# Window attention and two expert layers on one core: transposes of the last five tiles moved from TensorE to VectorE, late steps' square moved to ScalarE, new ranks for late work

## The chip, the cores and the metric

The kernel runs on one core of a Trainium2 chip. The time is that of one launch on the device in microseconds (us). Three runs of the kernel before gave 839.98, 840.34 and 841.68; 840.34 is their median. PE is TensorE, DVE VectorE, ACT ScalarE, POOL GpSimd, and SP the engine whose queue issues the DMA transfers. A core has one of each, each works through its own queue in order, and they wait for each other by semaphores.

## The reference

```python
def _attn_ref(q, k, v):                     # 4 x 8 x 576 x 64
    scores = scale * np.matmul(q, k.transpose(0, 1, 3, 2))
    mask = (rel >= 0) & (rel < 64)          # each query sees its own key and the 63 before
    scores = np.where(mask, scores, -1e9) - max
    attn = np.exp(scores); attn = attn / (attn.sum(-1) + 1e-09)
    return np.matmul(attn, v)

x = attn_out.transpose(0, 2, 1, 3).reshape(2304, 512)
h = x @ w_in; r = np.maximum(h, 0.0); x = (s * (r * r) + b) @ w_out    # 512 -> 2048 -> 512
h = x @ w_in2; out = np.maximum(0.01 * h, h) @ w_out2                  # 512 -> 2048 -> 512
```

The weights come as 64-bit floats, and the kernel turns their two 32-bit words into 32-bit floats itself.

## The kernel before, in words

*Attention.* The 2304 tokens are 18 tiles of 128. For a tile, TensorE computes the scores of two groups of four heads (`scores`, buffers sc), VectorE adds the mask and takes the row maximum (`mask_max`, eight instructions of 128 columns), ScalarE takes exp with the row sum (`exponent`), VectorE inverts the sum, and the rows are scaled (`normalise`). The result, called p, lies with queries on partitions (s, or in later tiles a part of the buffer vs). The product with v needs keys on partitions, so TensorE transposes p, four 128 x 128 blocks a group (`transpose_pe`, L285 to L288, into tp), ScalarE copies tp into pt (`take_transposed`, L290 to L296), and TensorE multiplies (`values`, L305, into xps). A tile's product stands in its queue whole (both groups next to each other) or in two halves.

*First layer.* Tokens are worked in blocks of 512, 512, 512, 512 and 256, and d_ff in 16 chunks of 128: 80 steps, each a pair of block and chunk. The first block's steps are cut in two runs of eight, with the second block's sixteen between them. Full precision comes from a split of every operand into a rounded high part and a remainder (h and l in the names: wh and wl, xh and xl, gh and gl) and three products of parts. A step has on TensorE twelve matmuls for h (`emit_h`, L532, into hps) and twelve for y (`emit_y`, L567, into acc, which gathers over the chunks in PSUM); between them come `activate` (L537 to L553): relu on ACT (L544, writes r), r = s*r*r on DVE (L546), gh = r + b rounded on ACT (L549), gl = r + b - gh on DVE (L551).

*Second layer.* Two levels of 2 x 2 blocks are multiplied with seven products each (L900, into xps, yps and zps), in three blocks of 768 tokens. Its weights are prepared during the first layer: 16 units (`add_weights2`, raw2 and flt2) are loaded, converted to 32-bit floats, summed and split on DVE and ACT, and stored to the DRAM buffers w1dr (first product) and w2dr (second), from which they are loaded again (ws).

*Order.* The program is written out by a planner (class `Order`): each operation has an engine, an estimated duration, the operations it waits for, the buffer rooms that it takes, and a key. Whenever a planned engine is free, the ready operation of the lowest key is emitted, so keys set the order in each queue. Keys are counted in steps: step s has keys near s, an attention tile has one key (L1157 for tiles 8 to 17) less an offset for each kind of operation, a weight unit of the second layer has STEPS1 - 10 or STEPS1 + 1 plus 0.1 for each unit (L1171; STEPS1 is 80). `fill` (L1122) puts matmuls of zeros (L1115, into warm or acc) where the planner sees TensorE idle in the first steps. What is in the queues is fixed when the program is built.

Of the kernel before, what the change touches and what calls it, by code (L numbers as in the profile page):

```python
# [9 lines left out]
F32 = mybir.dt.float32  # L10
# [116 lines left out]
def kernel(  # L127
# [82 lines left out]
    IN_W = (BLOCKS1[0] + BLOCKS1[1]) // P  # L210
    shared = {}
# [77 lines left out]

    def take_transposed(i, g):  # L290
        if i not in pt_t:
            pt_t[i] = (in_w("pt", [P, 2, H, D]) if i < IN_W
                       else tmpp.tile([P, 2, H, D], F32, tag="tmp", name="pt"))
        nc.scalar.activation(  # L294
            out=pt_t[i][:, :, 4 * g:4 * g + 4, :].rearrange("k a j q -> k j a q"),
            in_=tp_t[i, g].rearrange("k j (a q) -> k j a q", a=2), func=ACTF.Copy)  # L296
# [37 lines left out]
    def add_attention(i, b, t0, key):  # L334
# [3 lines left out]
        if i < IN_W:  # L338
            rq, rk, rv, first, rp = [mem("q")], [mem("k")], [mem("v")], [mem("s")], [mem("pt")]
            pt, after_v = ("pt", i), []  # L340
        else:
            rq, rk, rv, first, rp = [("q", "q", i)], [("k", "k", i)], [("big", "v", i)], [], [
                ("tmp", "pt", i)]
            pt, after_v = ("pt", i), [name("lv")]
# [15 lines left out]
        for g in range(2):  # L360
# [6 lines left out]
            for j in range(4):  # L367
                add(name("mm", g, j), "dve", 172, key - 4.87, lambda g=g, j=j: mask_max(i, g, j),
                    [name("sc", g)] + ([name("mm", 0, 0)] if g + j else after_v) + [("masks",)],
                    first if g + j == 0 else (), [("sc", i, j % 2), ss, ("sm", i)])  # L370
                add(name("exp", g, j), "act", 480, key - 3.07, lambda g=g, j=j: exponent(i, g, j),
                    [name("mm", g, j)], use=[ss, ("sm", i)])
# [12 lines left out]
            else:  # L385
# [4 lines left out]
            add(name("tp", g), "pe", 560, key - 2.96, lambda g=g: transpose_pe(i, g, tp),  # L390
                norm + [("masks",)], [(tp, "tp", i, g)], [ss])
            add(name("tt", g), "act", 478, key - 5.69, lambda g=g: take_transposed(i, g),
                [name("tp", g)] + ([name("tt", 0)] if g else []),
                [] if g else rp, [("tp", i, g), pt])
            last = [name("tt", g)]
# [140 lines left out]

    def activate(s, part):  # L537
        l, b, t0, n, c = steps[s]
        if part == 0:
            r_t[s] = gp.tile([P, NMAX], F32, tag="g", name="r")[:, :n]  # L540
            g_t[s] = tuple(gp.tile([P, NMAX], F32R, tag="g", name=t)[:, :n] for t in ("gh", "gl"))
        r, (gh, gl) = r_t[s], g_t[s]
        if part == 0:
            nc.scalar.activation(out=r, in_=hps_t[s], func=ACTF.Relu)  # L544
        elif part == 1:
            nc.vector.scalar_tensor_tensor(  # L546
                out=r, in0=r, scalar=sbt[:, 0:1], in1=r, op0=ALU.mult, op1=ALU.mult)
        elif part == 2:
            nc.scalar.activation(out=gh, in_=r, func=ACTF.Identity, bias=sbt[:, 1:2])  # L549
        else:  # L550
            nc.vector.scalar_tensor_tensor(  # L551
                out=gl, in0=r, scalar=sbt[:, 1:2], in1=gh.bitcast(F32), op0=ALU.add,
                op1=ALU.subtract)  # L553
# [49 lines left out]
    def add_step(s):  # L603
# [16 lines left out]
        add(("e", s, 1), "dve", 60 + 600 * f, s - 0.9, lambda: activate(s, 1),  # L620
# [518 lines left out]
    add(("masks",), "pool", 4000, -100, masks)  # L1139
    for c in range(KF):  # L1140
# [9 lines left out]
    for b, n in enumerate(BLOCKS1):  # L1150
        for j in range(n // P):
# [4 lines left out]
            else:  # L1156
                key = first_step[0, 2] - 10 + 2 * (i - IN_W)  # L1157
# [6 lines left out]
    for n, u in enumerate(units):  # L1164
# [6 lines left out]
        add_weights2(u, STEPS1 + (1 if u[1] else -10) + 0.1 * n, after)  # L1171
# [70 lines left out]
```

## Time and profile before

| | |
|---|---|
| median of three runs | 840.34 us |
| profiled execution, whole / span of its instructions | 838.37 / 836.6 us |
| granted TensorE clock, mean | 0.998 (of 2.4 GHz) |
| PE busy | 826.1 us, 99% |
| DVE busy | 600.5 us, 72% |
| ACT busy | 445.7 us, 53% |
| chain that ended last | PE 92%, DMA 2%, ACT 2%, DVE 2% |

The span runs from the first to the last instruction that the profiler shows; the execution is 1.8 us longer. Busy times of PE are from start to a modelled end, so two matmuls in a row overlap in them; what one costs is read from start to start. In the chain that ended last the matmuls of the first layer (L567 and L532) have 24% and 23%, those of the second (L900) 39%; the transposes of the tiles (L288) have 2% and their products with v (L305) 2%.

### The profile page before, as it was taken

Reading aid. Unit: us, or ns where it says so; the run is one execution under the profiler, and the core shown is the slowest. Engines: PE = TensorE matmul, PEld = TensorE weight load, DVE = VectorE, ACT = ScalarE, POOL = GpSimd, SP = SyncE. Lnnn points to the kernel's source line nnn. Section 1 sums busy time; section 2 is a strip of 40 time slices with the busy share of each in tenths; the row PEclk is TensorE's granted clock in tenths of the full one; section 3 lists DMA queues with packets and bytes.
Section 4 is the critical chain, followed back from the end, with each engine's and each line's share of the span. In section 5 each row is a group of like instructions: output and inputs, shape, how many; then the busy total and the mean of one; then the engine's idle time right before and its main releaser. Section 6 shows DMA issues by size and latency. Waiting matters only on the chain.

```text
span 836.6 us, 14149 instructions
## 1 busy us (share of the span) xinstructions
PE 826.1 (99%) x5289; PEld 735.7 (88%) x5289; DVE 600.5 (72%) x1095; ACT 445.7 (53%) x960; POOL 3.5 (0%) x13
## 2 busy tenths in 40 slices
PE   7999999999999999999999999999999999999998
PEld 4677888877777788888889999999999999999998
DVE  5999998556565756776878876699456688365963
ACT  5999655466776776443446433356332355222443
POOL 1000000000000000000000000000000000000000
PEclk9999999999999999999999999999999999999999
DMA  9763544438478564757388489899977898988783
GB/s 314 290 234 112 191 156 154 138 114 284 140 233 265 160 205 152 260 180 238 108 290 274 152 282 386 277 314 288 318 255 249 269 312 285 293 253 251 251 265 114
DMA packets 85909, 194.65 MB, mean 233 GB/s; under 512 B 7121, under 2 KB 50129, under 8 KB 81873
## 3 DMA queue, kind: packets, MB, share of 16 engines
q1 hardware_dynamic: 85840, 193.75, 69.7%
q8 instruction: 42, 0.69, 0.3%
q14 instruction: 27, 0.21, 0.1%
HBM read 151.26 MB, written 42.47 MB: 232 GB/s over the span
## 4 chain that ended last, share of the span: by engine, by line
PE 92%; DMA 2%; ACT 2%; DVE 2%; issue 1%; SPq 0%; ACTq 0%
PE acc L567 24%; PE hps L532 23%; PE xps L900 22%; PE zps L900 12%; PE yps L900 5%; PE xps L305 2%; PE sc L249 2%; PE tp L288 2%; DMA w2dr<-raw 1%; DMA x2l<-ydr 1%; DMA kt<-in_k 1%; PE warm L1115 1%; ACT pt L294 0%; DVE x2s L827 0%; ACT s L267 0%
## 5 line engine op out<-in xcount | busy, mean ns | idle before, releaser
L567 PE MATMUL acc<-gh,wh 128*128 128x512 f32 (+1 forms) x320 | 118.1, 375 | 0.0
L532 PE MATMUL hps<-xh,wh 128*128 128x512 f32 (+1 forms) x324 | 117.6, 370 | 0.1
L532 PE MATMUL hps<-xl,wh 128*128 128x512 f32 (+1 forms) x324 | 116.4, 367 | 0.0
L567 PE MATMUL acc<-gh,wl 128*128 128x512 f32 (+1 forms) x320 | 116.2, 369 | 0.0
L900 PE MATMUL xps<-x2h,ws 128*128 128x384 f32 x384 | 106.1, 334 | 0.4 <-ACT part L923 0.4
L796 ACT ACTIVATE g2s<-g 128x768 fp32r<-128x768 f32 x84 | 70.9, 847 | 64.0 <-PE xps L900 40.4
L923 ACT ACTIVATE part<-xps 128x384 f32<-128x384 f32 x90 | 44.1, 490 | 110.1 <-PE xps L900 110.0
L799 DVE TENSOR_TENSOR g2s<-g,g2s 128x768 fp32r<-128x768 f32 x84 | 80.1, 954 | 31.5 <-ACT g2s L796 30.7
L900 PE MATMUL xps<-g2s,ws 128*128 128x384 f32 x576 | 102.3, 334 | 0.1
L900 PEld LDWEIGHTS xps<-g2s,ws 128*128 128x128 f32 x576 | 99.9, 188 | 0.7 <-ACT part L923 0.7
L546 DVE SCALAR_TENSOR_TENSOR r<-r,sbt 128x512 f32<-128x512 f32 (+1 forms) x80 | 55.3, 691 | 44.0 <-ACT r L544 43.5
L567 PE MATMUL acc<-gl,wh 128*128 128x512 f32 (+1 forms) x320 | 86.1, 373 | 0.0
L544 ACT ACTIVATE r<-hps 128x512 f32<-128x512 f32 (+1 forms) x80 | 44.1, 551 | 78.6 <-PE hps L532 78.4
L532 PE MATMUL hps<-xh,wl 128*128 128x512 f32 (+1 forms) x324 | 80.6, 370 | 0.0
L551 DVE SCALAR_TENSOR_TENSOR gl<-r,sbt,gh 128x512 fp32r<-128x512 f32 (+1 forms) x80 | 55.5, 694 | 26.7 <-ACT gh L549 26.5
L532 PEld LDWEIGHTS hps<-xh,wh 128*128 128x128 f32 x324 | 61.1, 189 | 11.5 <-ACT wh L487 0.9
L900 PEld LDWEIGHTS xps<-x2h,ws 128*128 128x128 f32 x384 | 70.1, 188 | 0.7 <-ACT part L923 0.7
L567 PEld LDWEIGHTS acc<-gh,wh 128*128 128x128 f32 x320 | 60.3, 189 | 11.6 <-DVE st L594 0.7
L532 PEld LDWEIGHTS hps<-xl,wh 128*128 128x128 f32 x324 | 61.1, 189 | 9.8
L567 PEld LDWEIGHTS acc<-gh,wl 128*128 128x128 f32 x320 | 60.4, 189 | 9.4
L549 ACT ACTIVATE gh<-r,sbt 128x512 fp32r<-128x512 f32 (+1 forms) x80 | 54.0, 674 | 26.0 <-DVE r L546 26.0
L567 PEld LDWEIGHTS acc<-gl,wh 128*128 128x128 f32 x320 | 56.5, 189 | 10.7 <-issue 0.9
(93 smaller groups left out, 1395.9 us busy)
## 6 DMA issues: line engine op xcount, KB each, us to landing
ws<-w1dr SPq DMA_DIRECT2D x84, 512.0 KB, 4.6
ws<-w2dr SPq DMA_DIRECT2D x84, 512.0 KB, 4.6
raw<-in_w SPq DMA_DIRECT2D x31, 1024.0 KB, 5.1
w1dr<-raw SPq DMA_DIRECT2D x16, 512.0 KB, 5.0
w2dr<-raw SPq DMA_DIRECT2D x16, 512.0 KB, 4.1
kt<-in_k SPq DMA_DIRECT2D x14, 384.0 KB, 5.0
vs<-in_v SPq DMA_DIRECT2D x10, 512.0 KB, 3.8
out<-st SPq DMA_DIRECT2D x24, 192.0 KB, 4.2
```

The source lines that it names most:

```text
L249: nc.tensor.matmul(out=sc_t[i][r][D * a:D * a + D, p, :], lhsT=q_t[i][D * r:D * r + D, p, D * a:D * a + D], rhs=k_t[i][D * r:D * r + D, p, ...
L288: nc.tensor.transpose(tp_t[i, g][:, j, :], s_t[i][:, g, j, :], ident)
L532: nc.tensor.matmul(out=hps_t[s][:, c0:c1], lhsT=w[:, 0, kk * P:kk * P + P], rhs=x[l, b][:, kk, c0:c1], start=(kk == 0 and j == 0 and part ...
L544: nc.scalar.activation(out=r, in_=hps_t[s], func=ACTF.Relu)
L546: nc.vector.scalar_tensor_tensor(out=r, in0=r, scalar=sbt[:, 0:1], in1=r, op0=ALU.mult, op1=ALU.mult)
L549: nc.scalar.activation(out=gh, in_=r, func=ACTF.Identity, bias=sbt[:, 1:2])
L551: nc.vector.scalar_tensor_tensor(out=gl, in0=r, scalar=sbt[:, 1:2], in1=gh.bitcast(F32), op0=ALU.add, op1=ALU.subtract)
L567: nc.tensor.matmul(out=acc_t[r, m], lhsT=three[j][0], rhs=three[j][1], start=(c == c0 and j == 0), stop=(c == c1 - 1 and j == 2))
L796: nc.scalar.activation(out=out, in_=in_, func=ACTF.Copy)
L799: nc.vector.tensor_tensor(out=out, in0=in_, in1=hi.bitcast(F32), op=ALU.subtract)
L900: nc.tensor.matmul(out=out, lhsT=w_[:, wcut], rhs=x_, start=(opens and j == k == 0), stop=(j == n - 1 and k == 2), skip_group_check=not opens)
L923: nc.scalar.activation(out=t, in_=bank_t[(*key, "x")], func=ACTF.Copy)
```

## The change

Four things change. For tiles 13 to 17 (`BY_32 = 13`) p is transposed on VectorE: 24 instructions a tile, each of which transposes a strip of 32 queries by 32 keys for four heads, straight into one pt buffer that the five tiles share. The blocks that the mask leaves at zero aren't transposed; their places are set to zero once on POOL (`clear`). TensorE's transposes and ScalarE's copies of these tiles go. From step 46 on (`BY_ACT`) the square and the scale with offset are two ScalarE instructions, gh is a copy, and gl a plain subtraction on VectorE. Late tiles get other keys and other offsets of their operations, and the second layer's weight units too. The diff shows the new functions and each changed place.

```diff
@@ -281,6 +282,24 @@
...
+    def clear():
+        shared["pt"] = tmpp.tile([P, 2, H, D], F32, tag="tmp", name="pt")
+        for u in range(2):
+            nc.gpsimd.memset(shared["pt"][96 - 96 * u:128 - 96 * u, :, :, 32 * u:32 * u + 32], 0.0)
+    def transpose32(i, g, a, u, kb):
+        pt = pt_t[i] = shared["pt"]
+        q0 = D * a + 32 * u
+        nc.vector.transpose(
+            out=pt[32 * kb:32 * kb + 32, a, 4 * g:4 * g + 4, 32 * u:32 * u + 32],
+            in_=s_t[i][q0:q0 + 32, g, :, 32 * kb:32 * kb + 32])
@@ -365,10 +384,10 @@
...
-                add(name("mm", g, j), "dve", 172, key - 4.87, lambda g=g, j=j: mask_max(i, g, j),
+                add(name("mm", g, j), "dve", 172, key - (4.87 if early else 3.631), lambda g=g, j=j: mask_max(i, g, j),
-                add(name("exp", g, j), "act", 480, key - 3.07, lambda g=g, j=j: exponent(i, g, j),
+                add(name("exp", g, j), "act", 480, key - (3.07 if early else 3.369), lambda g=g, j=j: exponent(i, g, j),
@@ -387,12 +406,26 @@
...
-            add(name("tp", g), "pe", 560, key - 2.96, lambda g=g: transpose_pe(i, g, tp),
-                norm + [("masks",)], [(tp, "tp", i, g)], [ss])
-            add(name("tt", g), "act", 478, key - 5.69, lambda g=g: take_transposed(i, g),
-                [name("tp", g)] + ([name("tt", 0)] if g else []),
-                [] if g else rp, [("tp", i, g), pt])
-            last = [name("tt", g)]
+            if i < BY_32:
+                add(name("tp", g), "pe", 560, key - (2.96 if early else 2.594),
+                    lambda g=g: transpose_pe(i, g, tp),
+                    norm + [("masks",)], [(tp, "tp", i, g)], [ss])
+                add(name("tt", g), "act", 478, key - (5.69 if early else 1.5),
+                    lambda g=g: take_transposed(i, g),
+                    [name("tp", g)] + ([name("tt", 0)] if g else []),
+                    [] if g else rp, [("tp", i, g), pt])
+                last = [name("tt", g)]
+            else:
+                last = []
+                for u in range(2):
+                    for a in range(2):
+                        for kb in range(u, u + 3):
+                            n = name("t32", g, u, a, kb)
+                            add(n, "dve", 202, key - 7.437,
+                                lambda g=g, u=u, a=a, kb=kb: transpose32(i, g, a, u, kb),
+                                norm + [("clear",)]
+                                + [("pv", i - 1, h) for h in range(2) if i > BY_32], (), [ss, pt])
+                            last.append(n)
@@ -542,15 +578,24 @@
...
+        elif s < BY_ACT:
+            if part == 1:
+                nc.vector.scalar_tensor_tensor(
+                    out=r, in0=r, scalar=sbt[:, 0:1], in1=r, op0=ALU.mult, op1=ALU.mult)
+            elif part == 2:
+                nc.scalar.activation(out=gh, in_=r, func=ACTF.Identity, bias=sbt[:, 1:2])
+            else:
+                nc.vector.scalar_tensor_tensor(
+                    out=gl, in0=r, scalar=sbt[:, 1:2], in1=gh.bitcast(F32), op0=ALU.add,
+                    op1=ALU.subtract)
-            nc.vector.scalar_tensor_tensor(
-                out=r, in0=r, scalar=sbt[:, 0:1], in1=r, op0=ALU.mult, op1=ALU.mult)
+            nc.scalar.activation(out=r, in_=r, func=ACTF.Square)
+            nc.scalar.activation(
+                out=r, in_=r, func=ACTF.Identity, scale=sbt[:, 0:1], bias=sbt[:, 1:2])
-            nc.scalar.activation(out=gh, in_=r, func=ACTF.Identity, bias=sbt[:, 1:2])
-        else:
-            nc.vector.scalar_tensor_tensor(
-                out=gl, in0=r, scalar=sbt[:, 1:2], in1=gh.bitcast(F32), op0=ALU.add,
-                op1=ALU.subtract)
+            nc.scalar.activation(out=gh, in_=r, func=ACTF.Copy)
+        else:
+            nc.vector.tensor_tensor(out=gl, in0=r, in1=gh.bitcast(F32), op=ALU.subtract)
@@ -617,7 +662,8 @@
...
-        add(("e", s, 1), "dve", 60 + 600 * f, s - 0.9, lambda: activate(s, 1),
+        add(("e", s, 1), "dve" if s < BY_ACT else "act", 60 + (600 if s < BY_ACT else 1080) * f,
+            s - 0.9, lambda: activate(s, 1),
@@ -1137,6 +1183,8 @@
...
+    add(("clear",), "pool", 800, 0, clear, [("pv", BY_32 - 1, g) for g in range(2)],
+        [("tmp", "pt")])
@@ -1154,7 +1202,8 @@
...
-                key = first_step[0, 2] - 10 + 2 * (i - IN_W)
+                key = first_step[0, 2] + (
+                    2.0 * (i - IN_W) - 10.85 if i < BY_32 else 2.8 + 2.49 * (i - BY_32))
@@ -1168,7 +1217,7 @@
...
-        add_weights2(u, STEPS1 + (1 if u[1] else -10) + 0.1 * n, after)
+        add_weights2(u, STEPS1 + (3.5 if u[1] else -20.66) + 0.1 * n, after)

```

The offsets with `early` in them hold for tiles 4 to 17, since early are only tiles 0 to 3; so tiles 4 to 7, whose key stays, move too.

**TensorE between h of step 1 and the first y.** hps is h of step 1, tp the transposes of tile 4, xps its product with v, warm a matmul of zeros, acc the first y. Before:

```order
L532 MATMUL hps_634<-xl_410,wh_619 128x512
L288 MATMUL tp_654<-ident_94,s_479 128x128 x4
L532 MATMUL hps_634<-xh_409,wl_644 128x512 x4
L288 MATMUL tp_677<-ident_94,s_479 128x128 x4
L305 MATMUL xps_687<-pt_671,vt_432 64x64 x16
...
L1115 MATMUL warm_121<-zeros_95 128x512
...
L1115 MATMUL warm_121<-zeros_95 128x512
L567 MATMUL acc_726<-gh_663,wh_393 128x512
L567 MATMUL acc_726<-gh_663,wl_419 128x512
```

And now:

```order
L565 MATMUL hps_631<-xl_410,wh_619 128x512
L565 MATMUL hps_631<-xh_409,wl_642 128x512 x4
...
L1161 MATMUL warm_121<-zeros_95 128x512
...
L1161 MATMUL warm_121<-zeros_95 128x512
L612 MATMUL acc_701<-gh_657,wh_393 128x512
L612 MATMUL acc_701<-gh_657,wl_419 128x512
L612 MATMUL acc_701<-gl_658,wh_393 128x512
```

Between the last matmul of h and the first y there were eight transposes, tile 4's product and six matmuls of zeros; now there are 18 matmuls of zeros, and tile 4's transposes stand behind y.

**VectorE around tile 14's p.** vs holds p, sc the scores, r and gl are those of first-layer steps, flt2 and raw2 belong to a weight unit of the second layer; nothing of a transpose stands there before:

```order
L546 SCALAR_TENSOR_TENSOR r_2977<-r_2977,sbt_96 128x512
L464 SCALAR_TENSOR_TENSOR flt2_2958<-raw2_2902,flt2_2958 128x1024
L261 ISA vs_2964,nmax_3005<-sc_2984,mask_93 128x128
...
L551 SCALAR_TENSOR_TENSOR gl_2979<-r_2977,sbt_96,gh_2978 128x512
L468 SCALAR_TENSOR_TENSOR flt2_2958<-raw2_2902,flt2_2958 128x1024
L698 TENSOR_TENSOR raw2_2902<-flt2_2958 128x256
...
L546 SCALAR_TENSOR_TENSOR r_3055<-r_3055,sbt_96 128x512
L698 TENSOR_TENSOR raw2_2902<-flt2_2958,raw2_2902 128x256
L727 TENSOR_TENSOR flt2_2958<-flt2_2958,raw2_2902 128x512
L727 TENSOR_TENSOR flt2_2958<-flt2_2958,raw2_2902 128x256
L551 SCALAR_TENSOR_TENSOR gl_3057<-r_3055,sbt_96,gh_3056 128x512
```

And now, further on in the same unit, with pt the buffer that the five tiles share:

```order
L583 SCALAR_TENSOR_TENSOR r_2997<-r_2997,sbt_96 128x512
L773 TENSOR_TENSOR flt2_2887<-flt2_2887,raw2_2830 128x512
L300 STREAM_TRANSPOSE pt_2600<-vs_2904 32x4x32 x24
L588 SCALAR_TENSOR_TENSOR gl_2999<-r_2997,sbt_96,gh_2998 128x512
L583 SCALAR_TENSOR_TENSOR r_3055<-r_3055,sbt_96 128x512
L773 TENSOR_TENSOR flt2_2887<-flt2_2887,raw2_2830 128x256
```

The 24 block transposes stand in one piece between r of a step and its gl.

**TensorE at tile 14's product.** hps are h of two steps, xps is the product with v, acc are y of an earlier step; now:

```order
L565 MATMUL hps_3011<-xh_2467,wl_1041 128x512 x4
L565 MATMUL hps_3042<-xh_2467,wh_1133 128x512
...
L565 MATMUL hps_3042<-xl_2468,wh_1133 128x512
L324 MATMUL xps_3064<-pt_2600,vs_2904 64x64 x8
L612 MATMUL acc_2695<-gh_2998,wh_958 128x512
...
L565 MATMUL hps_3042<-xh_2467,wl_1149 128x512 x4
L324 MATMUL xps_3064<-pt_2600,vs_2904 64x64 x8
L612 MATMUL acc_2695<-gl_2999,wh_958 128x512
```

The product stands in two halves, one behind eight matmuls of h, one behind that h's last four; no transposes stand ahead of it.

## Rows read from the trace of the kernel before

**Rows 1.** The page, busy time of each engine, its share of the span, instructions.

```profile
PE 826.1 (99%) x5289; PEld 735.7 (88%) x5289; DVE 600.5 (72%) x1095; ACT 445.7 (53%) x960; POOL 3.5 (0%) x13
```

**Rows 2.** Waits of PE: line, releaser, us in total, times, longest.

```profile
PE xps L900 <- ACT part L923: 0.4, 1, 0.4
```

**Rows 3.** Busy us by stretch: PE, PEld, DVE, ACT, POOL, clock, DMA, GB/s.

```profile
238.00:322.00 84.00, 84.00 (x648) 66.45 (x647) 52.27 (x153) 59.50 (x174) 0.00 (x0) 1.00 0.60 196
322.00:433.00 111.00, 111.00 (x490) 91.56 (x489) 81.49 (x122) 49.43 (x77) 0.00 (x0) 1.00 0.64 213
```

**Rows 4.** The chain that ended last: start, length, line and count.

```profile
106.81 2.72 PE hps L532 x12
443.41 1.44 PE hps L532 x12
```

**Rows 5.** Timeline of PE, start of the first layer: start, length, line, tiles.

```profile
38.40 0.50 PE L532 MATMUL hps<-xh,wh 128*128 128x512 f32 x1
...
40.36 0.63 PE L288 MATMUL tp<-ident,s 128*128 128x128 f32 x4
...
42.29 1.49 PE L305 MATMUL xps<-pt,vt 128*64 128x64 f32 x32
43.71 1.47 PE L1115 MATMUL warm<-zeros 128*128 128x512 bf16 x6
44.83 0.58 PE L567 MATMUL acc<-gh,wh 128*128 128x512 f32 x1
```

**Rows 6.** Timeline of PE, transposes and product of tile 16.

```profile
301.13 0.39 PE L532 MATMUL hps<-xl,wh 128*128 128x512 f32 x1
301.36 1.03 PE L288 MATMUL tp<-ident,vs 128*128 128x128 f32 x8
...
302.70 0.40 PE L567 MATMUL acc<-gh,wh 128*128 128x512 f32 x1
...
303.85 0.39 PE L567 MATMUL acc<-gh,wl 128*128 128x512 f32 x1
...
306.37 1.10 PE L249 MATMUL sc<-kt,qt 64*64 64x128 f32 x32
```

**Rows 7.** Timeline of PE, tile 13's first transposes and a half product.

```profile
249.25 1.20 PE L288 MATMUL tp<-ident,vs 128*128 128x128 f32 x4
...
253.86 0.39 PE L567 MATMUL acc<-gl,wh 128*128 128x512 f32 x1
...
255.37 0.39 PE L567 MATMUL acc<-gl,wh 128*128 128x512 f32 x1
```

**Rows 8.** Timeline of DVE, two masked maxima in a row.

```profile
37.73 0.29 DVE L261 CUSTOM_DVE_ANT_0 s<-sc,mask 128x128 f32<-128x128 f32 x1
37.94 0.28 DVE L261 CUSTOM_DVE_ANT_0 s<-sc,mask 128x128 f32<-128x128 f32 x1
```

**Rows 9.** Groups by line and shape: busy us, mean ns | idle before, releaser.

```profile
L551 DVE SCALAR_TENSOR_TENSOR gl<-r,sbt,gh 128x512 fp32r<-128x512 f32 x64 | 47.8, 747 | 25.4 <-ACT gh L549 25.4
L546 DVE SCALAR_TENSOR_TENSOR r<-r,sbt 128x512 f32<-128x512 f32 x64 | 47.6, 744 | 39.6 <-ACT r L544 39.3
L544 ACT ACTIVATE r<-hps 128x512 f32<-128x512 f32 x64 | 38.0, 593 | 63.6 <-PE hps L532 63.4
...
L464 DVE SCALAR_TENSOR_TENSOR flt<-raw,flt 128x1024 uint32<-128x1024 uint32 x16 | 19.5, 1222 | 0.3
...
L698 DVE TENSOR_TENSOR raw<-flt 128x256 f32<-128x256 f32 x32 | 13.4, 418 | 0.2
...
L549 ACT ACTIVATE gh<-r,sbt 128x256 fp32r<-128x256 f32 x16 | 8.0, 503 | 5.1 <-DVE r L546 5.1
```

**Rows 10.** Issues at w2dr: count, ns min/median/max, first and last start.

```profile
L888 SPq DMA_DIRECT2D ws<-w2dr x84: 319/319/603, 527.7 to 816.5; - x84
L735 SPq DMA_DIRECT2D w2dr<-raw x32: 333/374/1037, 365.2 to 511.3; - x32
```

**Rows 11.** Timeline of ACT, start of the second layer; idle before and releaser.

```profile
507.41 0.85 ACT L796 ACTIVATE g2s<-g 128x768 fp32r<-128x768 f32 x1 [2.76 <-DMA w2dr<-raw]
```

More of the change, by code (lines that the diff above doesn't have):

```diff
@@ L210 @@
     IN_W = (BLOCKS1[0] + BLOCKS1[1]) // P
+    BY_32 = 13
     shared = {}
@@ L288, in transpose_pe @@
             nc.tensor.transpose(tp_t[i, g][:, j, :], s_t[i][:, g, j, :], ident)
+    def clear():
[8 more added lines that the diff above has]
+            in_=s_t[i][q0:q0 + 32, g, :, 32 * kb:32 * kb + 32])
+    def transpose_pe(i, g, tag):
+        tp_t[i, g] = ps[tag].tile([P, 4, P], F32, tag=tag, name="tp")
+        for j in range(4):
+            nc.tensor.transpose(tp_t[i, g][:, j, :], s_t[i][:, g, j, :], ident)
     def take_transposed(i, g):
@@ L343, in add_attention @@
                 ("tmp", "pt", i)]
-            pt, after_v = ("pt", i), [name("lv")]
+            pt, after_v = ("pt", i) if i < BY_32 else ("pt",), [name("lv")]
         cuts = ((0, 2), (2, 4)) if early else ((0, 4),)
@@ L535, in emit_h @@
                     stop=(kk == KD - 1 and part == 1))
+    BY_ACT = 46
     def activate(s, part):
```

## The prediction, made before the changed kernel was run

> **What bounds the kernel now.** I read the page first, then who waits for whom, then busy time by stretch, then the chain, and last the timeline of TensorE alone. The page has PE busy in 99% of the span and DVE in 72% [rows 1]. The list of waits shows that this is no artefact: behind the first 45 us the matmul queue has one listed wait, 0.4 us on an ACT copy in the second layer [rows 2]. In the two stretches that hold the changed tiles PE is busy for all 84 and all 111 us at full clock, DVE for 52 and 81 [rows 3]. The chain shows twelve 512-wide matmuls in 2.72 us, so 0.227 us from start to start, and twelve 256-wide ones in 1.44 [rows 4]. So the time is the sum of what stands in TensorE's queue, and each edit is priced by what it takes out of that queue, puts into it, or makes it wait for. DVE or ACT time counts only where PE comes to wait.
>
> A group of other matmuls between 512-wide ones is priced thus: from the start of the last one ahead to a start behind, less 0.227 for each wide one between. The eight transposes of tile 16 run from 301.13 to 302.70 over three wide ones: 0.89 us. Its p times v, whole, with five wide ones, from 303.85 to 306.37: 2.52, less 1.14 and the 0.09 that belongs to the score group behind, 1.29 [rows 6]. Half of one (tile 13's second), 253.86 to 255.37 over three: 0.83; so a product in two halves costs 1.66, 0.37 over a whole one [rows 7]. The transposes are 128-wide float32 and the rows show each group of four costing 0.45.
>
> **Tiles 13 to 17, transposes.** Forty transposes leave PE. Four tiles give 0.89 each. Tile 13's first four took 1.20 us in the timeline where another four took 0.63 [rows 5, 7]; I read the difference as a wait for the normalisation ahead of them, and that tile gives 0.89 + 0.57. Together -5.0. In the new order all five p times v stand in halves; before, tiles 13 to 15 did and 16 and 17 stood whole, so +0.7. The ten ACT copies out of PSUM go as well, but ACT isn't waited for there: nothing.
>
> **Tiles 8 to 12.** Their groups stay but stand differently: tiles 9 and 11 get whole products and tile 10 a split one, at 0.37 each: -0.4.
>
> **The start.** Here the ranks cost time. In the order before, the idle stretch ahead of the first y holds tile 4's eight transposes, its product and six fillers; in the one after it holds 18 fillers and nothing else, and tile 4's work stands behind. The old stretch runs from 38.40 (h of step 1) to 44.83 (first y) [rows 5]. The new one: 0.1 us of start and twelve wide matmuls, 41.2, then 18 fillers; six take 1.47 us less 0.23 of overlap, about 0.225 each [rows 5], so 4.1: y starts at 45.3, 0.5 later. The 0.89 and 1.29 of tile 4 then come on top, and tile 5's split product 0.4, while some 0.3 us in which the old y waited between its first matmuls go: about +2.7. Bounds: if the fillers hide wholly, +2.2; if DVE, which now does three weight-conversion steps ahead of the first r, brings gl later than 45.8, +4. Nothing absorbs this later, since PE has no idle time behind it.
>
> **Block transposes on DVE.** 24 in a tile, 120 in all, each 32 partitions by 128 elements. No row shows one. The nearest by size is the masked maximum, 128 elements too, from start to start 0.21 us [rows 8]; the next is a 256-element sum, 0.418 [rows 9]. I take 0.24, near the first, since 128 elements are what it streams: 5.8 us a tile; the ends are 0.20 and 0.42. What is queued behind them is the next gl and r, and TensorE waits for both those and the pt that they write. For tile 13 the new PE order does two h ahead of y, so even 0.42 is hidden. The tight one is tile 14. PE, from the end of y 34 to tile 14's first half product, has y 35, y 36, h 38 and eight matmuls of h 39: 3 x 2.72 + 1.82 = 10.0 us [rows 4]. DVE can't begin before y 34 is done, since r of step 36 takes the buffers that it frees. It then has: relu on ACT 0.59, two r of 0.74, eight maxima 1.7, gl 0.75, one conversion of 1.22, four sums of 0.42 [rows 8, 9], less 0.08 of overlap for each of the long ones, together about 6.8, a 512-wide subtraction and two small ones about 1.0 (an estimate, from gl's 0.75), and twelve block transposes, 2.9: 10.7 to 10.9. PE waits 0.9. Done the same way, tiles 15 to 17 have 1 to 3 us to spare. So +0.9; with 0.20 it is +0.4, with 0.42 a tile gets 4.3 us longer and four of them overrun, +8.
>
> **Square and offset on ACT, from step 46.** DVE loses one r of 0.74 in each of 34 steps and gl becomes a plain subtraction. DVE isn't waited for there, so this gains nothing by itself. ACT gets two instructions more. Steps of 512 have 5.44 us and stay clear. Those of 256 have 2.88 [rows 4] for relu, square, scale-and-offset and copy, at most 0.50 each by the old gh [rows 9]: 2.0 in a row on one engine. gh is wanted 2.88 us behind its h, so 0.8 is left: nothing, up to +1 where weight splits stand between.
>
> **The second layer's weights and start.** The weight units of the second layer get other ranks: those of its first product earlier by 10.66 steps, those of its second later by 2.5. With them move each unit's load and stores on SP's queue and its conversions, sums and splits on DVE and ACT. Earlier ones can only be ready sooner, and DVE has room for them. For the later ones the cover is this: the last store of the second product's weights is issued at 511.3, the first load of them at 527.7 [rows 10], so 16 us lie between, and 2.5 steps are at most 13.6. I cost it at nothing; beyond the 16 us PE would wait for what is late, microsecond for microsecond, and a store that waits at the head of SP's queue holds up the loads behind it. The 0.4 us wait [rows 2] came from a g2s copy that stood on ACT ahead of the awaited one and waited 2.76 us for a weight store [rows 11]. In the new order this copy stands some 7 us later, behind more of the awaited copies: -0.4, or nothing if it meets another store. The zeroing on POOL is off every path.
>
> **Sum.** -5.0 + 0.7 - 0.4 + 2.7 + 0.9 - 0.4 = -1.5 us. The profiled execution took 838.37 (span 836.6), which becomes 836.9. The runs shown have a median of 840.34, 2.0 above it; against that the forecast is 838.8.
>
> **Rivals.**
> *The block transposes are slow and TensorE waits.* At 0.42 DVE needs 10 us a tile; first late is tile 14's pt, then 15 to 17, +8 instead of +0.9: 846. It decides from about 0.29 on, where tile 14 alone costs 1.5 and the rest are at their margin (839.5). For it: the 419 ns row, and a stretch in which DVE, at 73% before, gets 20 us more. Against it: 128 elements took 0.21.
> The Trainium skill (VectorE: DVE Perf Modes, "Rules for kernel authors" and "The three transpose paths") advises TensorE for a 128 x 128 transpose into PSUM and VectorE only for blocks of 32, and gives 311 ns for VectorE on a 128 x 128 tile; by that, as an estimate, a tile takes 7.5 us and the whole would come out near 840. No row here shows the operation.
> *The start costs nothing.* If tile 4's deferred work meets waits that PE has in any case, or the tile-14 wait isn't there, 2 us of the costs go: 836.8. Against it: no idle time is listed behind 45 us.
> *ACT's chain in the 256-wide steps.* gh comes late in some of sixteen steps, each by up to 0.3: +2.5, 841.3. For it: the four are in line on one engine, with x splits between in steps 68 to 72; against it the 0.8 us of room.
>
> **How the numbers follow.** Forecast 0.50 (its own range 837.3 to 840.3), slow transposes 0.17, cheap start 0.15, ACT chain 0.10, something unseen 0.08, split evenly. A measurement of this kernel tells 0.2%, 1.7 us, from no change; 840.34 less that is 838.66, so the forecast sits just inside "same": of its half, 0.22 falls to faster, 0.28 to same. Faster: 0.22 + 0.15 + 0.04 = 0.41. Same: 0.28 + 0.02 of the slow transposes + 0.05 of the ACT chain = 0.35. Slower: 0.15 + 0.05 + 0.04 = 0.24. The range, 836.0 to 844.0, takes in the cheap start, the ACT chain and transposes up to about 0.34 us.
>
> **What would show it.** First y at 45.3 with 18 fillers ahead; h and y from there to step 7 about 2.7 us behind; no tp matmul behind 250 us; block transposes 0.20 to 0.29 from start to start; one wait of PE of about 1 us at an xps near step 39; no ACT wait at 508. Wrong if the transposes take 0.35 or more, if PE waits at several xps, or if the first y starts before 45.

## The result and the profile after

The changed kernel is slower: 845.90 us median over 15 runs (842.32 to 850.18) against 840.23 for the kernel before, measured again beside it (836.47 to 844.12). The ratio is 1.0069, with a 95% interval of 1.0050 to 1.0089. The profiled execution took 843.57 us, with a span of 841.4, 4.8 over the span before (836.6). Both profiled executions are shorter than the median of their kernel, by 1.9 us before and by 2.3 now.

The first line of the page after, busy time by engine:

```profile
PE 827.1 (98%) x5261; PEld 733.7 (87%) x5261; DVE 617.0 (73%) x1181; ACT 480.6 (57%) x1018; POOL 4.5 (1%) x15
```

PE's busy time has not fallen, though 40 transposes left its queue: twelve more matmuls of zeros stand in it (18 take 4.06 us below, six took 1.47 [rows 5]), and a busy time that runs to a modelled end hides part of what PE loses. What shows the loss is the list of waits. Before, it held one entry behind the first 45 us [rows 2]. Now (releaser; us in total, times, longest):

```profile
PE acc L612 <- ACT st L641: 1.9, 1, 1.9
...
PE acc L612 <- DVE st L639: 1.0, 2, 0.8
...
PE xps L946 <- ACT part L969: 0.9, 2, 0.6
...
PE xps L324 <- DVE pt L300: 0.5, 1, 0.5
PE acc L612 <- DVE gl L588: 0.4, 2, 0.2
PE acc L612 <- ACT gh L596: 0.4, 1, 0.4
```

The two largest are a kind that the prediction did not have: y of a new run of steps needs a PSUM bank, and the copy that empties it (`leave`, into st) comes late. The chain that ended last says why. Its DMA steps at the ends of runs (start, length); the chain before has no DMA step between 10 and 499 us:

```profile
95.87 7.35 DMA ydr<-st
...
196.51 6.21 DMA ydr<-st
...
348.87 6.37 DMA xdr<-xo
356.08 4.99 DMA ydr<-st
```

Steps 0 to 7, 8 to 23, 24 to 31 and so on are runs; the first, second and fourth end near 100, 200 and 355 us, and there four banks are copied out through two staging buffers. A copy waits until a store has landed. At 348.87 the store is that of an attention tile's output, xo, which uses the same two buffers. The copies behind it, from the timelines of DVE and ACT (idle before and releaser in brackets):

```profile
355.36 0.69 DVE L639 COPY st<-acc 128x512 f32<-128x512 f32 x1 [1.30 <-DMA xdr<-xo]
361.14 0.60 ACT L641 ACTIVATE st<-acc 128x512 f32<-128x512 f32 x1 [1.39 <-DMA ydr<-st]
```

Before, a copy at 354.88 waited for a store as well, 2.03 us, but PE didn't wait for it.

To see where the time went I took the same matmul (the n-th of h, y and the second layer's products) in both traces and subtracted its start times; the step in that difference at a place is what the place cost. The eleven rows add up to 4.65 of the 4.8 us.

| place | forecast | measured |
|---|---|---|
| start, to 98 us | +2.7 | +2.2 |
| end of the first run, 98 to 105 | not in the sum | +0.8 |
| tiles 8 to 12, whole or split | -0.4 | -0.35 |
| end of the second run, 202 | not in the sum | +0.95 |
| gh late at 240 | not in the sum | +0.3 |
| 40 transposes gone | -5.0 | -5.05 |
| split products of tiles 13 to 17 | +0.7 | +0.7 |
| waits for pt and gl in these tiles | +0.9 | +1.7 |
| end of the fourth run, 355 to 362 | not in the sum | +2.3 |
| gh late in the 256-wide steps, 458 to 470 | 0 | +1.0 |
| second layer's start | -0.4 | +0.1 |
| sum | -1.5 | +4.7 |

These are the sizes in one pair of executions. The kernels of e2, e3, e4, e9, e11 and e12 below have the changed kernel's order up to 239 us. In their executions, in this order, the first run's end cost 1.7, 0.35 and then four times nothing, and the second's 0.9 to 1.7. So the +0.8 is for the most part this one execution's, and the loss at the second run's end is in all of them.

The start, from the timeline of PE, answers to [rows 5]:

```profile
40.94 4.06 PE L1161 MATMUL warm<-zeros 128*128 128x512 bf16 x18
44.65 0.58 PE L612 MATMUL acc<-gh,wh 128*128 128x512 f32 x1
...
47.61 1.03 PE L307 MATMUL tp<-ident,s 128*128 128x128 f32 x8
```

The first y starts at 44.65 and not at 45.3 (h of step 1 came 0.46 earlier); the eight transposes of tile 4 stand behind it, as forecast. The block transposes and the new ScalarE instructions, by line and shape, answer to [rows 8, 9]:

```profile
L300 DVE STREAM_TRANSPOSE pt<-vs 32x128 f32<-32x128 f32 x120 | 36.3, 303 | 6.3 <-ACT vs L279 4.4
...
L593 ACT ACTIVATE r<-r,sbt 128x256 f32<-128x256 f32 x16 | 9.6, 602 | 0.5
```

From start to start a block transpose takes 0.316 us in the trace, so a tile has 7.63 us in one piece (timeline of DVE, tile 16):

```profile
320.20 7.63 DVE L300 STREAM_TRANSPOSE pt<-vs 32x128 f32<-32x128 f32 x24 [0.46 <-ACT vs L279]
327.86 0.75 DVE L588 SCALAR_TENSOR_TENSOR gl<-r,sbt,gh 128x512 fp32r<-128x512 f32 x1
```

gl, which PE needs next, stands behind the 7.63 us. The prediction took 0.24 and the planner 0.24 too (202 ns and 40 for the wait).

### The profile page after: what moved, and what is told of

Its sections match the earlier page's. It is cut to its first block, busy times and chain, and to the rows that moved or that the text cites. A ratio compares the mean times of both kernels' runs of the same rounds, so it can differ in the third digit from the quotient of the medians.

```text
span 841.4 us, 14236 instructions
## 1 busy us (share of the span) xinstructions
PE 827.1 (98%) x5261; PEld 733.7 (87%) x5261; DVE 617.0 (73%) x1181; ACT 480.6 (57%) x1018; POOL 4.5 (1%) x15
## 4 chain that ended last, share of the span: by engine, by line
PE 79%; DVE 9%; DMA 6%; ACT 3%; issue 2%; SPq 0%; ACTq 0%; DVEq 0%
PE xps L946 24%; PE acc L612 17%; PE hps L565 17%; PE zps L946 12%; PE yps L946 6%; DVE pt L300 3%; DMA ydr<-st 2%; DMA xdr<-xo 2%; PE sc L250 1%; PE xps L324 1%; DMA w1dr<-raw 1%; PE tp L307 1%; DVE gl L588 1%; ACT vs L279 1%; DVE s L262 1%
## 5 line engine op out<-in xcount | busy, mean ns | idle before, releaser
L565 PEld LDWEIGHTS hps<-xh,wh 128*128 128x128 f32 x324 | 61.1, 189 | 11.2 <-ACT wh L520 0.5
L565 PEld LDWEIGHTS hps<-xh,wl 128*128 128x128 f32 x324 | 56.2, 189 | 10.4 <-issue 0.7
L946 PE MATMUL xps<-x2l,ws 128*128 128x384 f32 x192 | 64.1, 334 | 0.0
L972 DVE TENSOR_TENSOR g<-zps,part 128x384 f32<-128x384 f32 x48 | 26.7, 555 | 47.9 <-ACT part L969 28.6
```

The costliest lines, as they stand in the source:

```text
L565: nc.tensor.matmul(out=hps_t[s][:, c0:c1], lhsT=w[:, 0, kk * P:kk * P + P], rhs=x[l, b][:, kk, c0:c1], start=(kk == 0 and j == 0 and part ...
L946: nc.tensor.matmul(out=out, lhsT=w_[:, wcut], rhs=x_, start=(opens and j == k == 0), stop=(j == n - 1 and k == 2), skip_group_check=not opens)
L972: nc.vector.tensor_tensor(out=out, in0=bank_t[(*key, kind)], in1=copy_t[key, what], op=ALU.add)
```

## The experiments

In e1 and e3 a rotation gave out a buffer of the second layer's weights near 600 us before it had been read; their times past that are not used. e5 to e8, e10 and e12 have one edit more than is shown here: they give these buffers out by what is free. Differences are of profiled executions, by the same matmuls as above. Executions of one kernel differ by several us (the 15 of the changed kernel by 7.9), so a difference counts by its place, and a whole only by medians.

**e1, tiles 4 to 7 as before.** In the four ranks, as here:

```diff
-key - (4.87 if early else 3.631)
+key - (4.87 if i < IN_W else 3.631)
```

> The changed kernel, with the old offsets for tiles 4 to 7 (their operations' ranks as before the change); all else as changed. Theory (the loss is a sum of places: 2.2 us in the first 98 us, 0.8 at the end of the first run of steps near 100, 0.95 at the end of the second near 202, 2.3 at the end of the fourth near 358, 1.0 in the 256-wide steps near 460): the first 98 us take what they took before, and the copies out at the first run's end find their staging buffers free again, so the span falls from 841.4 by about 3.0 to 838.4; the wait near 358 stays, since tile 17's product still stands at the run's end. Rival (the start's delay only moves waits that come anyway at the run ends, where stores decide): it falls by 1 or less, 840.4 to 841.4.

At 95 us it is 2.7 us ahead of the changed kernel, at 107 us 3.6, at 364 us 5.2, at the end of the first layer 5.8: under the kernel before by 1.1. The theory holds for the start. It said that the wait near 358 stays, and that went too (2.1 us): in this order tile 17's product is done at 336 us and its output is stored at 338.7, long before the run ends. In the second layer, between 525 and 550 us, PE lost 11.2 us that nobody had expected, so the whole did not get faster.

**e2, square and offset on VectorE throughout.**

```diff
-BY_ACT = 46
+BY_ACT = 80
```

> The changed kernel, with square and offset back on VectorE in all steps. Theory: the waits for gh in the 256-wide steps near 460 to 470 go, 1.0 us, and nothing else moves much: span 840.4. Rival (the room that ScalarE's taking over leaves on VectorE is what the block transposes live from): VectorE comes late with pt or gl in steps 46 to 50 and near 358 to 365, and the span rises by 1 or more.

From 456 to 479 us it gains 1.0 on the changed kernel, as the theory said. Then it loses 7 us in the second layer, which neither side foresaw; span 849.0. This execution is 4.0 over the kernel's median, which is 1.0097 of the time before, about 2 us over the changed kernel's 1.0069.

**e3, other staging buffers at the fourth run's end.**

```diff
-return ("st", "st", "q", "k")[m] if runs[r][1] >= len(BLOCKS1) - 2 else "st"
+return ("st", "st", "q", "k")[m] if runs[r][1] >= len(BLOCKS1) - 3 else "st"
```

> The changed kernel, where two of the four copies out at the fourth run's end (near 356 us) go to the buffers of q and k, which no tile needs any more, and not to the two staging buffers that tile 17's output shares. Theory (PE waits there because a staging buffer is held by tile 17's output, whose store took 6.4 us, and by the copies ahead): the waits of 0.24 and 2.03 us go, span 839.1. Rival (the copies are late because ScalarE and VectorE are, or the stores' traffic holds up the loads behind): PE waits as long, for another releaser, span 841.4.

The waits near 358 are gone: from 350 to 364 us it gains 2.6. Its chain there is PE alone:

```profile
354.86 2.72 PE acc L612 x12
357.57 2.72 PE hps L565 x12
360.30 2.72 PE acc L612 x12
```

So the staging buffers held PE up. Three kernels that keep the buffers agree: in e1 and e4 tile 17's output is stored by 339 us, in e12 the run ends some 3 us later, and in all three at most 0.2 us is lost there. But at 240 us, ahead of any difference in its order, this execution lost 4.7 us more than the changed kernel's (below).

**e4, the transposes back on TensorE**, with the new keys as they were.

```diff
-BY_32 = 13
+BY_32 = 18
```

> The changed kernel, with the transposes of tiles 13 to 17 back on TensorE and ScalarE, at the new keys. Theory: PE gets 40 transposes back (+4.5), four split products fewer (-1.5), and loses the waits for pt and gl behind the block transposes (-1.7): +1.3, span 842.7, with the waits at the run ends about as they are. Rival (the block transposes on VectorE cost more than they save): span under 840.5.

Span 844.7, 3.3 over the changed kernel. Of this 1.0 stands at 240, ahead of any difference in order. From there to 352 us it loses 4.0, about the theory's 1.3 and two waits, 2.5 in all, for pt, a copy on ScalarE. At the fourth run's end it gains 2.1, which the theory did not have: tile 17's product is done at 337 us and not at 348, and the copies don't wait. So the move to VectorE saves PE's time in its stretch and, by making tile 17 late, loses half of that again. The medians don't tell the two kernels apart (1.0074 and 1.0069 of before). The rest of the change, without the transposes, is 6.6 us slower than before by its median.

**e5 and e6, e1 with the old ranks of the weight units; e6 with `BY_ACT = 80` too.**

```diff
-(3.5 if u[1] else -20.66)
+(1 if u[1] else -10)
```

> The changed kernel with the old offsets for tiles 4 to 7 and the old ranks of the second layer's weight units; the buffers of the second layer's weights are given out by what is free (in the first kernel of this kind a rotation gave one out before it was read). Theory (with tiles 4 to 7 as before, the first layer ends 1.6 us under before; the last weight units then come too late only because they were also ranked 2.5 steps later): the waits of PE from 525 to 555, 11 us in the kernel with the old offsets alone, shrink to under 2, span 835 to 837. Rival (the units are late because they may only begin when tile 17's product is done, four steps later than before the change, and their rank doesn't matter): waits of 5 to 11 us stay there, span 840 to 846.

> As the kernel before it (old offsets for tiles 4 to 7, old ranks of the weight units), and square and offset on VectorE in all steps. Theory: the waits for gh in the 256-wide steps go (0.4 to 1.0), and VectorE, which then has 25 us more to do from step 46 on, brings the weight units later, so that what is won there is lost near 530: span within 1 us of the kernel before it. Rival (VectorE has room to spare there): 0.5 to 1.0 us shorter than the kernel before it.

e5 ends the first layer 1.4 under before and e6 2.3 under; then they lose 11.3 and 14.5 us: spans 846.5 and 848.7. So e5's rival holds in its number, a little past its range: the rank doesn't matter. Its reason, tile 17, does not hold (below). Of e6 neither side had the size: the 0.9 us of the first layer came, and the second layer costs 3 us more with the square on VectorE.

**e7 and e8, the block transposes alone on the kernel before; in e8 the planner reckons their true time.**

```diff
-add(n, "dve", 202,
+add(n, "dve", 276,
```

> The kernel before the change, with one part of the change: the block transposes of tiles 13 to 17 on VectorE. All ranks and offsets are the old ones, square and offset stand where they stood. Theory: the first 240 us as before; 40 transposes less on PE (-5.0), two more split products (+0.7), waits for pt and gl of 1 to 2 us; but a tile now goes round in 3 steps and not in 2.3, so tile 17's product comes at step 48 and not 44, the weight units begin four steps later, and PE waits for them between 510 and 560, by 2 us or more. Span 834.5 to 839 by the size of that wait. Rival (the units have 16 us of cover and a later tile 17 costs nothing): 833.0 to 834.5.

> As the kernel before it (before the change, with the block transposes alone), and the planner reckons 0.316 us for a block transpose, as measured, and not 0.242. Theory: the waits of PE for pt and gl in the tiles fall from 1 to 2 us to under 0.5, but the planner sees tiles later by another step, so tile 17's product moves to step 49 to 50 and the weight units' waits grow; the two cancel to within 1 us. Rival (the planner's error is what costs): 1 to 2 us shorter than the kernel before it.

Spans 851.7 and 850.4; ratios 1.021 and 1.019. The expectation of e7 misses by more than 10 us. e8 ends 1.3 under e7 (2.5 by the medians), past its theory and inside its rival's range; what its theory said of the parts, shorter waits in the tiles and later units, came too. The first layer of e7 is 2.9 us over before, of e8 0.5 (0.8 of the difference stands ahead of 100 us, 1.2 are shorter waits in the tiles); the second loses 12.3 and 13.3. PE's waits in e7 from 480 to 600 us:

```profile
PE xps L952 <- DMA ws<-w1dr: 4.6, 2, 2.8
PE xps L952 <- ACT part L977: 1.5, 3, 0.6
PE yps L952 <- DMA ws<-w1dr: 1.2, 1, 1.2
PE zps L952 <- DMA ws<-w1dr: 0.6, 1, 0.6
```

PE waits for weights (ws). The loads of the 16 weight units (raw; times: first and last issue) of before, changed kernel, e5 and e7, in this order:

```profile
L671 SPq DMA_DIRECT2D raw<-in_w x16: 328/345/668, 136.8 to 470.1; - x16
```

```profile
L717 SPq DMA_DIRECT2D raw<-in_w x16: 328/345/393, 137.2 to 476.2; - x16
```

```profile
L717 SPq DMA_DIRECT2D raw<-in_w x16: 328/334/661, 138.2 to 511.3; - x16
```

```profile
L717 SPq DMA_DIRECT2D raw<-in_w x16: 328/345/496, 137.4 to 516.7; - x16
```

Where the last unit's load is issued by 480 us, the second layer costs 3.0 or less over before (the changed kernel, e4, e9, e11, e12); where the last one alone comes at 500 or later, 4 to 7 (e2, e3, e10); where the last two do, 10.5 to 14.5 (e1, e5 to e8). The late units' loads and stores then share SP's queue with the ws loads. A unit's load waits in that queue until the stores of the unit two before it have landed, and the ws loads behind it wait too. SP's own waits in e7 from 480 to 560 us have:

```profile
SPq L717 <- DMA w2dr<-raw: 6.8, 2, 3.6
```

The kernels in which two units are late have two such waits there, 5.6 to 6.8 us together, e2, e3 and e10 one of 2.3 to 2.5, and before, the changed kernel, e4, e9, e11 and e12 none. What makes units late is open. Pairs of units may start when tile 17's product is done, at 320 us before; but that time doesn't decide. It is 336 in e1, e5, e6 and e10, where units are late, and 348 to 353 in the changed kernel, e9, e11 and e12, where none is, and in e2 and e3, where one is.

**e9, two thirds of the block transposes.** All of pt is set to zero once.

```diff
+        if kb == u + 2:
+            return
```

> The changed kernel with every instruction in its place, but 8 of a tile's 24 block transposes left out (the last strip of keys of each set of three stays zero, so p times v of tiles 13 to 17 lacks that part). A tile then has 2.5 us less on VectorE, as if a transpose took 0.21. Theory (the transposes cost by the waits for pt and gl that stand behind them, 1.7 us at 289, 327 to 329 and 343): these go and the rest stays, span 839.7, with the waits near 202, 240 and 358 about as they were. Rival (VectorE's time as a whole holds the stretch up): span 838 or less.

From 250 to 349 us it gains 1.7 on the changed kernel, and no wait for pt or gl is left; that settles what their duration costs directly. At the fourth run's end it gains another 1.0. The median is 841.81 (1.0035, interval 1.0016 to 1.0055), about 2.9 us under the changed kernel's share of before (1.0069), nearer to the rival's 3.4 than to the theory's 1.7. The profiled execution, span 844.0, is one with a long wait at 240.

**e10, e1 with pairs of weight units begun one unit sooner.**

```diff
-ALONE = 6
+ALONE = 5
```

> The changed kernel with the old offsets for tiles 4 to 7, the weights' buffers of the second layer given out by what is free, and pairs of weight units begun one unit earlier in their row (the seventh, not the eighth, is the first that waits for tile 17 and then runs beside another). Theory (where PE waits 9 to 14 us near 510 to 555 it waits for the last two weight units, whose loads are issued at 501 or later, and does not where both are issued by 476): one unit is now late instead of two, the waits there fall to 2 to 4 us, and the gain of the first layer stays: span 834.5 to 838. Rival (the waits there come from the traffic of loads and stores on SP's queue, however early a unit begins): 843 or more.

Span 840.2, ratio 1.0047 (1.0027 to 1.0066). One unit is late (load at 515.7), the second layer's loss falls to 4.2 and the first layer is 0.6 under before. The theory's direction holds; its span was missed by 2. It doesn't beat the kernel before.

**e11, the weight units' ranks alone** (the diff of e5 on the changed kernel).

> The changed kernel with the old ranks of the second layer's weight units alone. Theory: each unit waits for the one or two before it, so a rank changes little: the same span within what two executions of the changed kernel differ by, 840 to 843.5. Rival (the new ranks cost, by loads put ahead of stores on SP's queue near 200): 839.5 or less.

Span 847.1, in one execution, above both ranges. The second layer costs 0.7 over before, so the ranks change little there. Of the 5.7 us over the changed kernel 4.2 stand at 240 with the slower clock behind it (last section), 0.7 at 202 and 1.0 behind the last matmul, and its order is that of the changed kernel up to 368 us. Its ScalarE at 240 (the last column is the wait):

```profile
242.15 1.12 ACT L487 ACTIVATE flt<-raw 128x1024 f32<-128x1024 f32 x1 [3.10 <-DMA raw<-in_w]
243.16 0.71 ACT L586 ACTIVATE gh<-r,sbt 128x512 fp32r<-128x512 f32 x1
```

and the same in the changed kernel:

```profile
239.08 1.12 ACT L487 ACTIVATE flt<-raw 128x1024 f32<-128x1024 f32 x1 [2.05 <-DMA raw<-in_w]
240.11 0.71 ACT L586 ACTIVATE gh<-r,sbt 128x512 fp32r<-128x512 f32 x1
```

gh, for which PE waits, stands behind a conversion that waits for its load. Before, the conversion waited too, but no gh that PE needed soon stood behind it (one went ahead of it at 237.82, the next came at 251.14):

```profile
241.05 1.12 ACT L454 ACTIVATE flt<-raw 128x1024 f32<-128x1024 f32 x1 [2.50 <-DMA raw<-in_w]
```

Of six executions of this order (the changed kernel, e2, e3, e4, e9, e11) three lost about 3 us there, the others 1.3 or less. The load takes as long in both, 4.9 to 5.0 us from its issue (234.10 and 237.24) to the conversion; what differs is the issue. It waits at the head of SP's queue for a store of an earlier unit to land. SP's waits from 222 to 240 us, changed kernel and e11:

```profile
SPq L717 <- DMA w1dr<-raw: 7.9, 1, 7.9
```

```profile
SPq L717 <- DMA w1dr<-raw: 9.5, 1, 9.5
```

This wait is 7.3 to 8.6 us in the three short executions and 9.5 to 9.8 in the three long ones.

**e12, gh ahead of that conversion.**

```diff
-[name("cv2", part - 1)] if part else [name("lw2")],
+[name("cv2", part - 1)] if part else [name("lw2")] + ([("e", 30, 2)] if u == (3, 0) else []),
```

> The changed kernel, where the first conversion on ScalarE of the fourth weight unit stands behind gh of step 30 and not ahead of it (two more operations are exchanged behind it on their way). Theory (near 240 us gh waits behind that conversion, which waits for its load; the load lands now early, now late, so PE loses 0.3 us in one execution and 3 us, and after that half its clock for 5 us, in another): no wait for gh at 240 and no fall of the clock there, the time from 236 to 252 as in the shortest executions of the changed kernel, and a median under that of the changed kernel by 1 to 2.5 us, 843.5 to 845 where the changed kernel had 845.9. Rival (the load's lateness moves to the next thing that needs it): a median of 845.5 or more.

The wait at 240 went and the clock stayed up there, though the load was again issued late (SP waited 9.6 us). Another wait of 1.8 us came at 260: y behind `part` on VectorE, which had waited 3.45 us for its own load, from ydr. The median is 845.89, the changed kernel's, so the rival has the number. That the unit's lateness moved is not shown, since the load waited for at 260 is another one.

## Why the prediction was wrong

- *The failed step* is the rule that PE's queue alone sets the time, and that others count at tile 14 and the second layer's start only. The sum has no term for the copies at the runs' ends: +0.8, +0.95 and +2.3, 4.1 of the 6.3 us between forecast and profiled result. The order showed xo of a late tile and `leave` of four banks; that they share two buffers was to be read in the code. e3 shows it for the largest, and e1, e4 and e12 agree; for the second it is read off the chain alone; the first is absent in four other executions of the same order and so is not shown to come from the change. The sum has no term either for gh behind a conversion at 240, 0.3 us here and, with the slower clock behind it, 4.5 to 5.0 in three other executions.
- *Transposes and splits*: right to 0.1 us. e4 says that the move is worth 4.0 from 249 to 352 us and about 2 with the fourth run's end.
- *The start*: right, +2.2 for +2.7, and e1 gives it back. The first y came before 45, which the prediction had called a sign of being wrong; h of step 1 had started 0.46 earlier, which says nothing of the ranks.
- *Block transposes*: the value taken, 0.24, was too low; 0.316 lies inside the bounds, a little past the point (0.29) from which the rival was to decide. The wait came as that rival said, 1.7 us, in three tiles and not in one. The prediction's estimate from the 311 ns of the Trainium skill (VectorE: DVE Perf Modes, "The three transpose paths") was 7.5 us for a tile; the trace has 7.63. The Trainium skill has the 311 ns for a 128 x 128 tile of bf16 and not for a strip of 32 partitions in float32, so that the two agree may be chance.
- *What a late tile 17 does* was missed altogether: its product moves from 320 to 348 us and its output meets the fourth run's end. The longer tile and the new ranks both do it: it is 341 in e7, which has the block transposes alone, and 337 in e4, which has the rest without them. The cover of 16 us that the prediction read [rows 10] shrank to 7 in the changed kernel (count, ns, first and last start)

```profile
L934 SPq DMA_DIRECT2D ws<-w2dr x84: 319/319/807, 532.6 to 821.3; - x84
L781 SPq DMA_DIRECT2D w2dr<-raw x32: 359/371/1428, 383.4 to 525.7; - x32
```

  the last such store is issued at 525.7, the first load at 532.6. It held. What failed in eight of the other kernels was SP's queue: up to 600 us PE's waits for loads there were for ws<-w1dr, but for one of 1.6 us in e1, and the stores to w1dr were all issued by 381 us. The prediction had named such a queue, "a store that waits at the head of SP's queue holds up the loads behind it", and gave it no price; it was a unit's load that waited there.
- *ScalarE's chain in the 256-wide steps*: costed at nothing, with up to +1 "where weight splits stand between". It was +1.0. In the trace of ScalarE a split of a weight unit and one of x stand ahead of a step's four:

```profile
459.77 1.04 ACT L763 ACTIVATE raw<-raw 128x1024 fp32r<-128x1024 f32 x1
460.72 0.83 ACT L842 ACTIVATE x2h<-x2s 128x768 fp32r<-128x768 f32 x1
461.45 0.37 ACT L580 ACTIVATE r<-hps 128x256 f32<-128x256 f32 x1
461.85 0.42 ACT L592 ACTIVATE r<-r 128x256 f32<-128x256 f32 x1
462.31 0.60 ACT L593 ACTIVATE r<-r,sbt 128x256 f32<-128x256 f32 x1
462.94 0.42 ACT L596 ACTIVATE gh<-r 128x256 fp32r<-128x256 f32 x1
```

  so relu starts late and gh comes 0.5 late. e2 gives it back.
- *The second layer's start*: the wait at 508 went (0.4 in the list, 0.6 by the differences) and one of 0.7 at 522 came.
- *Range and chances*: 845.9 lies above 844.0. Slower had 0.24, and no rival held several small waits on buffers together.

Open: why the store that decides at 240 lands after 8 us in some executions and after 10 in others, and what makes the last weight units late in some orders. Nor was a kernel found that keeps what the move saves in its stretch and loses none of it.

## What to carry over

Where an engine is never idle, the time of work moved off it can be read from start to start (here 5.05 us for a forecast 5.0). The loss must be sought in what the new order delays: buffers that two users share, and whatever stands in a queue behind an instruction or a transfer that waits. When a tile ends later, or ranks change, look at each queue for what now stands behind a load, and at each shared buffer for who holds it then.

## What was not expected of the hardware

After some waits TensorE ran slower for a while. In e11 (columns: us, PE, PEld, DVE, ACT, POOL busy, granted clock, DMA share, GB/s) it was busy 1.23 of 4 us and had then a granted clock of 0.66:

```profile
240.00:244.00 4.00, 1.23 (x7) 0.67 (x5) 0.70 (x2) 1.85 (x3) 0.40 (x1) 1.00 0.98 383
244.00:249.00 5.00, 5.00 (x15) 3.95 (x16) 4.97 (x7) 1.15 (x3) 0.00 (x0) 0.66 0.05 21
249.00:253.00 4.00, 4.00 (x20) 3.30 (x19) 2.41 (x6) 1.69 (x4) 0.00 (x0) 1.00 0.19 66
```

Its 512-wide matmuls (timeline of PE) went on at 0.23 us from start to start for a microsecond and then at 0.43:

```profile
243.93 0.50 PE L612 MATMUL acc<-gh,wh 128*128 128x512 f32 x1 [2.77 <-ACT gh L586]
...
245.33 0.63 PE L612 MATMUL acc<-gh,wl 128*128 128x512 f32 x1
245.76 0.63 PE L612 MATMUL acc<-gh,wh 128*128 128x512 f32 x1
246.19 0.63 PE L612 MATMUL acc<-gh,wl 128*128 128x512 f32 x1
```

A clock of 0.66 over the five us is a part of them at the lower level, 1.2 GHz, and not half the clock for all five, as the expectation of e12 had it. So a wait of 2.8 us cost about 1.5 more (seven gaps of 0.2 and part of one).

The same came where weights were late. In e7:

```profile
528.00:535.00 7.00, 5.76 (x19) 5.66 (x19) 5.85 (x11) 2.65 (x5) 0.00 (x0) 0.52 1.03 376
```

So the 12.3 us of e7's second layer are more than the 7.9 us of its listed waits. In e12 a wait of 1.88 us at 522 was followed by a clock of 0.54 from 524.3 to 528 us; in e4 one of 2.37 us at 315 was followed by 1.00.
